# Attention's probabilities transposed by VectorE blocks and DRAM instead of TensorE, with the second half of each pair as a chain of its own

## The chip, the cores and the metric

One NeuronCore of a Trainium2 chip runs the whole program. The metric is the device time of one execution in microseconds; the median of three runs of the kernel before is 1203.68 us (1203.37 to 1203.94).

## What is computed

The reference has three stages; sizes are 2304 tokens (4 batches of 576), 512 features, 8 heads of 64.

```python
# 1. attention inside chunks of 64 tokens, for every head
scores = scale * np.matmul(q_c, k_c.transpose(0, 1, 2, 4, 3))
scores = scores - np.max(scores, axis=-1, keepdims=True)
attn = np.exp(scores)
attn = attn / (np.sum(attn, axis=-1, keepdims=True) + 1e-09)
out = np.matmul(attn, v_c)
# 2. four experts (512 -> 1024 -> 512), weighted by p and summed
h = np.maximum(x @ w1[e], 0.0)
out += p[:, e:e + 1] * (h @ w2[e])
# 3. rms norm, then a gated unit (512 -> 1536 -> 512)
g = xn @ w_gate
silu = g * (1.0 / (1.0 + np.exp(-g)))
val = xn @ w_val
return (silu * val @ w_out)
```

## The kernel before, in words

Tokens are cut into 18 tiles of 128, and these into three sets of six (`NSET`, `TPS`). Six stages follow each other on TensorE: the experts ("moe") for sets 0, 1 and 2, then the gated unit ("glu") for sets 0, 1 and 2. A moe stage has eight blocks k = 0 to 7 (four experts, two blocks each). A block is two calls of `hidden` (line 779: seven products of six 128x384 matmuls, in banks named a_ps, b_ps, c_ps, d_ps, with sums on VectorE between them) and one `outer` (line 942: six output tiles o, twelve 128x512 matmuls each, each tile added into `acc` by VectorE at line 1343). A glu stage has three blocks of four `hidden` and one `second` (line 977: seven `mult` of 18 matmuls 128x256; GpSimd and ScalarE make its operands, `part`). fp32 products are made of three passes over a high and a low part (`PASSES`).

Attention of set 0 runs at the start, one tile at a time. The twelve tiles of sets 1 and 2 run as six pairs beside the moe stages of sets 0 and 1 (`attention_unit`, line 481): load q, k and v; scores on TensorE into two PSUM banks sc; softmax, which takes nine VectorE instructions, two exponentials on ScalarE and four multiplications on GpSimd; then for each tile four 128x128 transposes on TensorE (line 529) into a bank trA, which ScalarE copies to SBUF as aT (line 534); then the products pv of aT with v (line 556), which ScalarE copies into xr (line 582). Set 2's pairs start at block (1, 4), that is k = 4 of the moe stage of set 1.

The order of all work is fixed when the program is built. `Chains` keeps a clock that `work.tick` moves on by an estimate of TensorE's time after each group of matmuls; each chain is a generator that is stepped when the clock reaches its next time, and `work.pause(us)` is a wait on this clock. `work.force` drives one chain to its end at once. On the chip every engine executes its own list in order, and all DMAs of interest go through one list, that of SyncE (SP below). Apart from attention these chains matter here:

- `weights` and `fetch` load and split expert weights; `w1_load` (line 299) loads parts of split weights into the twelve slots of `w1p`. `store` and `store_q` (lines 280, 457) put split parts away in DRAM, and on SP they wait for the GpSimd subtraction that makes the part.
- `decode` (lines 393 to 424) makes fp32 from the 64-bit gate, value and output weights with six VectorE instructions and one GpSimd addition per tile; its raw loads (`fetch64`, line 388) wait on SP for the VectorE instruction that frees their buffer. `prepare` splits the decoded tiles.
- `spot(n)` (line 773) puts one VectorE instruction of `decode` (or of `x_sums`, when that is under way) at places between TensorE groups. During blocks (1, 4) to (1, 7) a flag `busy` leaves out the spots that aren't marked calm.
- `put_away` and `turn` (lines 1175, 1192) already transpose the normalised expert output in another way: one VectorE instruction transposes a 128x512 tile in blocks of 32x32 (line 1181), four DMAs put the blocks in place in DRAM (`blocks_out`, line 1164, pieces of 32 rows), and a later load brings them back.

At the last block of a moe stage, line 1316 forces the attention chain to its end before `hidden` goes on.

## Time and profile before

| | us |
|---|---|
| runs, median (lowest to highest) | 1203.68 (1203.37 to 1203.94) |
| the profiled execution, its own time | 1204.62 |
| its span, first to last instruction | 1202.8 |
| TensorE matmul busy | 1188.5 (99%) |
| VectorE, ScalarE, GpSimd busy | 838.0, 482.7, 724.3 |
| DMA queue q1, share of 16 engines | 75.0% |

The profiled execution took 0.94 us more than the median; its span leaves out 1.8 us around the first and last instruction. The busy share of TensorE is an upper bound, since matmuls overlap and their ends are modelled: what one costs is read from the distance between starts. A wait is shown with the engine and line that ended it.

### The profile page before, as it was taken

How to read it: one execution, taken by the hardware profiler on the slowest of the kernel's cores; microseconds unless marked ns; L12 is line 12 of the kernel's file. 1: busy time of each engine (PE TensorE's matmuls, PEld its weight loads, DVE VectorE, ACT ScalarE, POOL GpSimd, SP SyncE). 2: the span in 40 equal slices, each digit the busy share in tenths (PEclk: the TensorE clock that was granted, in tenths of full speed). 3: DMA queues.
4: the chain of work that ended last, by engine and by line, in shares of the span. 5: the costliest groups of instructions: out<-in, count | busy, mean ns of one | idle time of the engine just before them, and what ended most of it. 6: DMA issues, size and time to landing. Idle time of an engine off the chain costs nothing.

```text
span 1202.8 us, 22161 instructions
## 1 busy us (share of the span) xinstructions
PE 1188.5 (99%) x7668; PEld 1109.1 (92%) x7668; DVE 838.0 (70%) x1456; ACT 482.7 (40%) x1116; POOL 724.3 (60%) x776
## 2 busy tenths in 40 slices
PE   8999999999999999999999999999999999999998
PEld 7888889999999988899999999999999999999998
DVE  5765544457678877779779888885687646774657
ACT  6445443333234334433344333344724243244322
POOL 4697666664476736547767776666337645385344
PEclk9999999999999999999999999999999999999999
DMA  8477655554679998576879998847998897688685
GB/s 262 145 265 248 232 193 201 193 189 149 208 243 322 321 311 293 185 242 203 287 257 305 294 304 298 307 169 238 315 289 252 290 323 239 228 282 294 216 292 178
DMA packets 190432, 302.47 MB, mean 251 GB/s; under 512 B 55280, under 2 KB 62960, under 8 KB 190320
## 3 DMA queue, kind: packets, MB, share of 16 engines
q1 hardware_dynamic: 189744, 300.53, 75.0%
q8 instruction: 61, 1.00, 0.3%
q10 hardware_dynamic: 576, 0.52, 0.1%
q14 instruction: 51, 0.42, 0.1%
HBM read 229.15 MB, written 71.83 MB: 250 GB/s over the span
## 4 chain that ended last, share of the span: by engine, by line
PE 91%; POOL 3%; DVE 2%; issue 1%; ACT 1%; DMA 1%; SPq 0%; DVEq 0%; POOLq 0%; ACTq 0%
PE o L956 30%; PE c_ps L726 14%; PE a_ps L726 14%; PE d_ps L726 14%; PE b_ps L726 7%; PE x L1006 7%; PE y L1006 3%; POOL w L201 1%; POOL tw L201 1%; PE pv L556 1%; DMA v<-in_qkv 1%; POOL hl L201 1%; PE sc L505 1%; PE trA L529 0%; ACT x L711 0%
## 5 line engine op out<-in xcount | busy, mean ns | idle before, releaser
L956 PE MATMUL o<-w,hh 128*128 128x512 f32 x1152 | 357.3, 391 | 0.6 <-POOL w L201 0.6
L201 POOL TENSOR_TENSOR w<-r,w 128x512 fp32r<-128x512 f32 (+1 forms) x146 | 168.9, 1164 | 151.1 <-ACT w L361 55.9
L956 PEld LDWEIGHTS o<-w,hh 128*128 128x128 f32 x1152 | 214.6, 188 | 44.2 <-POOL w L201 1.4
L956 PE MATMUL o<-w,hl 128*128 128x512 f32 x576 | 224.4, 390 | 0.0
L726 PE MATMUL c_ps<-x,w 128*128 128x384 f32 x1080 | 215.9, 337 | 1.0 <-DVE d_ps L202 1.0
L726 PE MATMUL a_ps<-x,w 128*128 128x384 f32 x984 | 198.0, 337 | 0.5 <-ACT p L787 0.5
L726 PE MATMUL d_ps<-x,w 128*128 128x384 f32 x984 | 197.2, 336 | 0.0
L726 PEld LDWEIGHTS c_ps<-x,w 128*128 128x128 f32 x1080 | 189.1, 188 | 2.0 <-DVE d_ps L202 1.6
L726 PEld LDWEIGHTS a_ps<-x,w 128*128 128x128 f32 x984 | 172.5, 188 | 3.3 <-ACT p L787 1.0
L726 PEld LDWEIGHTS d_ps<-x,w 128*128 128x128 f32 x984 | 173.0, 188 | 0.0
L1343 DVE SCALAR_TENSOR_TENSOR acc<-o,pr,acc 128x512 f32<-128x512 f32 x126 | 93.7, 747 | 111.9 <-PE o L956 111.8
L201 POOL TENSOR_TENSOR hl<-silu,hh 128x384 fp32r<-128x384 f32 x50 | 51.8, 1056 | 130.3 <-ACT hh L865 130.3
L956 PEld LDWEIGHTS o<-w,hl 128*128 128x128 f32 x576 | 108.1, 188 | 22.7
L201 POOL TENSOR_TENSOR w<-tw,w 128x256 fp32r<-128x256 f32 x136 | 112.5, 837 | 6.4 <-ACT w L236 5.9
L787 ACT COPY p<-a_ps 128x384 f32<-128x384 f32 x82 | 39.3, 480 | 155.0 <-PE a_ps L726 154.8
L726 PE MATMUL b_ps<-x,w 128*128 128x384 f32 x492 | 98.6, 336 | 0.0
L201 POOL TENSOR_TENSOR hl<-h_s,hh 128x384 fp32r<-128x384 f32 x70 | 73.8, 1076 | 40.3 <-ACT hh L865 20.8
L827 ACT ACTIVATE hh<-d_ps 128x384 fp32r<-128x384 f32 x92 | 45.3, 492 | 130.8 <-DVE d_ps L202 130.5
L202 DVE TENSOR_TENSOR u<-b_ps,p 128x384 f32<-128x384 f32 x82 | 45.4, 554 | 74.7 <-PE b_ps L726 54.3
L202 POOL TENSOR_TENSOR w<-w,sc 128x512 f32<-128x512 f32 x36 | 50.9, 1415 | 75.1 <-DVE sc L420 74.4
L236 ACT CAST w<-tw 128x256 fp32r<-128x256 f32 x136 | 51.9, 405 | 102.5 <-POOL tw L201 100.7
L1006 PE MATMUL x<-w,hh 128*128 128x256 f32 x480 | 91.3, 283 | 0.4 <-ACT x L711 0.4
(142 smaller groups left out, 1956.4 us busy)
## 6 DMA issues: line engine op xcount, KB each, us to landing
w<-wgv SPq DMA_DIRECT2D x252, 256.0 KB, 4.8
w<-w1m SPq DMA_DIRECT2D x224, 256.0 KB, 5.1
r<-in_w SPq DMA_DIRECT2D x128, 256.0 KB, 4.9
w<-wou SPq DMA_DIRECT2D x63, 512.0 KB, 5.9
w1m<-w SPq DMA_DIRECT2D x112, 256.0 KB, 3.2
wgv<-w SPq DMA_DIRECT2D x84, 256.0 KB, 4.8
raw<-in_wglu SPq DMA_DIRECT2D x36, 512.0 KB, 4.6
wou<-w SPq DMA_DIRECT2D x42, 256.0 KB, 3.9
```

What stands on the lines that cost most here:

```text
L201: sub = lambda eng, o, a, b: eng.tensor_tensor(o, a, b, op=ALU.subtract)
L202: add = lambda eng, o, a, b: eng.tensor_tensor(o, a, b, op=ALU.add)
L236: nc.scalar.copy(halves(out[n])[:, 0], at[part_of[n]])
L505: nc.tensor.matmul(sc[h2][c * CH:(c + 1) * CH, n:n + CH], q, k, start=True, stop=True)
L556: nc.tensor.matmul(ps[n][lo:lo + CH, o:o + CH], vt[a][row:row + CH, hp, c, :], aT[a][row:row + CH, q:q + CH], start=True, stop=True,)
L726: nc.tensor.matmul(ps[:, :NB], wv[:, wi, k, :], xs[n][:, xi, k, :], start=(first and k == 0 and m == 0), stop=(last and k == KH - 1 and m ...
L787: nc.scalar.copy(p1, v(a))
L827: nc.scalar.activation(hi, src, AF.Relu)
L956: nc.tensor.matmul(ps, hs[fps[k], b, j][hx][:, r * P:(r + 1) * P], w2[2 * k + j][:, wi], start=((k, j, m) == (0, 0, 0)), stop=((k, j, m) = ...
L1006: nc.tensor.matmul(ps[:, o:o + w], parted[fps[q], n][hx][:, t * P:(t + 1) * P], wv[:, q, wi], start=id(ps) not in opened, stop=(n in (1, 2 ...
L1343: nc.vector.scalar_tensor_tensor(out=acc[i], in0=ps, scalar=pr[:, i, e:e + 1], in1=acc[i], op0=ALU.mult, op1=ALU.add,)
```

## The change

The first six tiles keep the old way (`turned_here`). For the other twelve:

- VectorE transposes the tile of probabilities in 32x32 blocks into aq (one 128x512 instruction), four DMAs put the blocks into a new DRAM tensor `attd[i]` (pauses of 0.8 us between them instead of the 1.6 us of the other user), and a DMA loads aT from there.
- The load and what follows (pv and its copies) are a chain of their own, `attention_end`, so the next pair's scores can start before the pair has ended. It waits 2.5 us on the clock, loads the two aT, then waits 8 us more before pv.
- `placed=True`: a step of attention that wants VectorE is no longer taken when the clock is due; it is taken by `spot`, ahead of `decode`. The flag `busy` and the calm spots are gone. The row sums and the following two small instructions of softmax are now two steps.
- Set 2's pairs start at block (1, 2) instead of (1, 4), and `prepare` is slowed from there.
- At the last block of a moe stage, `force` also ends every chain in `ending`.
- In the very last `second`, three of the six closing additions go to GpSimd and all six are issued before `mult(1)`.

```diff
@@ -78,9 +78,9 @@
     def __init__(self):
         self.clock, self.rush, self.chains = 0.0, False, []
 
-    def add(self, gen, every=0.0, first=False, busy=None):
-
-        c = [gen, every, self.clock, every if busy is None else busy]
+    def add(self, gen, every=0.0, first=False, busy=None, placed=False):
+
+        c = [gen, every, self.clock, every if busy is None else busy, placed, None]
         self.chains.insert(0, c) if first else self.chains.append(c)
         return c
 
@@ -92,15 +92,18 @@
     def step(self, c, busy=False):
         c[2] = max(c[2], self.clock - 2.0) + c[3 if busy else 1]
         try:
-            next(c[0])
+            c[5] = next(c[0])
         except StopIteration:
             self.chains.remove(c)
+
+    def due(self, c):
+        return c[4] and c[5] is not None and "DVE" in c[5][0]
 
     def tick(self, us, busy=False):
         self.clock += us
         for c in list(self.chains) if not self.rush else ():
             for _ in range(2):
-                if c in self.chains and self.clock >= c[2]:
+                if c in self.chains and self.clock >= c[2] and not self.due(c):
                     self.step(c, busy)
 
     def race(self, runners, spare, idle):
@@ -182,6 +185,7 @@
     w1p = Slots(tc, ctx, "w1", 12, [P, 2, 2 * P], F32R)
     w2p = Slots(tc, ctx, "w2", 4, [P, 2, 512], F32R)
     r64 = Slots(tc, ctx, "r64", 2, [P, 1024], F32)
+    attd = {i: dram.tile([KD, P, P], F32, name=f"att_{i}") for i in range(TPS, NTILE)}
     xnt = [dram.tile([KD, P, NB], F32, name=f"xnt_{b}") for b in range(2 * NSET)]
     away = set()
     psum = ctx.enter_context(tc.tile_pool(name="psum", bufs=1, space=PSUM))
@@ -520,6 +524,23 @@
         yield from work.pause(5)
 
         aT = []
+        if done:
+            yield from turned_here(u, att, aT)
+            yield from attention_out(u, loaded, aT, d, done)
+            return
+        qs = []
+        for i, t in zip(u, att):
+            while not tp.free():
+                yield
+            yield {"DVE": 0.7}, 1
+            qs.append(tp.get(f"aq_{i}"))
+            nc.vector.transpose(qs[-1], t)
+            tp.put(t)
+            yield from work.pause(1.5)
+            yield from blocks_out(qs[-1], attd[i], 0, 0.8)
+        ending.append(work.add(attention_end(u, loaded, qs, aT, d)))
+
+    def turned_here(u, att, aT):
         for a, t in enumerate(att):
             yield {"PE": 0.45}, 1 + 2 * a
             while banks.free() < (1 if work.rush else 3) or not tp.free():
@@ -533,6 +554,22 @@
             yield {"ACT": 0.6}, 1
             nc.scalar.copy(aT[a], ps)
             banks.put(ps)
+
+    def attention_end(u, loaded, qs, aT, d):
+        yield from work.pause(2.5)
+        for i in u:
+            while not tp.free():
+                yield
+            aT.append(tp.get(f"aT_{i}"))
+            nc.sync.dma_start(out=aT[-1].rearrange("p (k n) -> p k n", k=HP), in_=attd[i].rearrange("k p n -> p k n"))
+            yield from work.pause(1)
+        yield from work.pause(8)
+        tp.put(*qs)
+        yield from attention_out(u, loaded, aT, d, None)
+
+    ending = []
+
+    def attention_out(u, loaded, aT, d, done):
         yield from work.pause(1)
         yield {"PE": 1.05 * len(u)}, 1
 
@@ -609,9 +646,10 @@
         yield {"ACT": d}, 1
         nc.scalar.activation(ex[1][:, :G * CH], ex[1][:, :G * CH], AF.Exp, scale=SCALE)
         for h2, e in enumerate(ex):
-            yield {"DVE": d + 0.6}, 3 - h2
+            yield {"DVE": d}, 3 - h2
             rs = sm.tile([P, G, 1], F32, tag="rs", name=f"rs_{h2}")
             nc.vector.tensor_reduce(rs, rows(e), axis=AX.X, op=ALU.add)
+            yield {"DVE": 0.6}, 1
             nc.vector.tensor_scalar_add(rs, rs, 1e-9)
             nc.vector.reciprocal(rs, rs)
             yield {"POOL": 0.65 * len(att)}, 1
@@ -768,13 +806,16 @@
             made_plain.pop(0)()
             catch_up()
 
-    decoding, adding, summing_up, busy = [], [], [False], [False]
-
-    def spot(n, calm=False):
-        for c in adding[-1:] if adding and adding[-1] in work.chains else decoding * (n if calm or not busy[0] else 0):
-            for _ in range(1 + summing_up[0]):
+    decoding, adding, summing_up = [], [], [False]
+
+    def spot(n):
+        for _ in range(n):
+            for c in adding[-1:] + [c for c in work.chains if work.due(c)] + decoding:
                 if c in work.chains:
                     work.step(c)
+                    if c in decoding and summing_up[0]:
+                        work.step(c)
+                    break
 
     def hidden(key, use):
 
...
@@ -1086,9 +1127,12 @@
         aside(2)
         spot(2)
         if last:
-            for o, y in (("c22", "y1"), ("c21", "y2")):
-                plus(nc.vector, o)
-                plus(nc.vector, y, high)
+            plus(nc.vector, "c22")
+            plus(nc.gpsimd, "c21")
+            plus(nc.vector, "y1", high)
+            plus(nc.gpsimd, "c12")
+            plus(nc.vector, "y2", high)
+            plus(nc.gpsimd, "y3", high)
             write("c22", both, 0, 1, (0, 1))
             write("y1", high, 0, 1, (2,), nc.scalar)
         mult(1, 0, 0, 0)
@@ -1099,8 +1143,6 @@
         spot(2)
         if last:
             take("y2", small[0], both)
-            plus(nc.vector, "c12")
-            plus(nc.vector, "y3", high)
             write("c11", both, 1, 0, (0, 1))
             write("y2", low, 1, 0, (2,), nc.scalar)
         mult(3, 6, 2 if last else 0, 1)
@@ -1161,7 +1203,7 @@
 
     scaled = []
 
-    def blocks_out(t, where, at):
+    def blocks_out(t, where, at, gap=1.6):
 
         rows = where.rearrange("k (j r) n -> r (k j) n", r=SQ)
         for g in range(P // SQ):
@@ -1169,7 +1211,7 @@
                 out=rows[:, :, at + g * SQ:at + (g + 1) * SQ],
                 in_=t[g * SQ:(g + 1) * SQ].rearrange("r (m c) -> r m c", c=SQ),
             )
-            yield from work.pause(1.6)
+            yield from work.pause(gap)
             yield
 
     def put_away(tiles):
@@ -1294,8 +1336,8 @@
                 if moe and (s, k) == (0, 1) and resting in work.chains:
                     work.force(resting, lambda: resting not in work.chains)
                 room[0] = 6 if k == 0 else 8 if k >= len(plan) - 2 else 0
-                if moe and (s, k) in ((0, 1), (1, 4)):
-                    ahead = work.add(attention(own(s + 1)), first=True)
+                if moe and (s, k) in ((0, 1), (1, 2)):
+                    ahead = work.add(attention(own(s + 1)), first=True, placed=True)
                 if (moe and s > 0 and k == 2) or (not moe and (s, k) == (0, 1)):
                     work.add(norm(s - 1 if moe else NSET - 1), 1.5)
                 if moe and s == 0 and k == 1:
@@ -1304,16 +1346,20 @@
                     work.add(fetch64())
                     decoding.append(work.add(decode(), 1e9))
                     preparing = work.add(prepare(), 1.0)
-                if moe and (s, k) in ((1, 4), (2, 0)):
-                    busy[0] = s == 1
+                if moe and (s, k) in ((1, 2), (2, 0)):
                     preparing[1] = 1.5 if s == 1 else 0.9
                 if k == len(plan) - 2 and not final:
                     if ahead is None:
                         ahead = work.add(turn(0 if moe else s + 1), 1.0)
                 if end and not final:
                     hold[0] = True
-                    if ahead in work.chains:
-                        work.force(ahead, lambda: ahead not in work.chains)
+                    for c in [ahead] + ending:
+                        if c in work.chains:
+                            work.force(c, lambda: c not in work.chains)
+                    for c in ending:
+                        if c in work.chains:
+                            work.force(c, lambda: c not in work.chains)
+                    ending.clear()
                     summing = work.add(x_sums((5,) if moe else (5, 6, 2)), 1e9 if moe else 0.8)
                     if moe:
                         work.step(summing)
```

`hidden` and `outer` lose the calm argument of `spot` and are otherwise unchanged. How this moves instructions is shown at three places.

TensorE, before: the end of the last `hidden` of block (1, 6) and the start of its `outer`, with the transposes (trA) of the last pair, tiles 16 and 17. In these names w is a part of the weights, x the split input, o an output tile, at the probabilities.

```order
L726 MATMUL d_ps<-x_3720,w_2_6118 128x384 x6
L726 MATMUL c_ps<-x_3732,w_3_6129 128x384 x6
L529 MATMUL trA_6346<-ident,at_6200 128x128 x4
L956 MATMUL o_6364<-w_6140,hh 128x512 x2
L956 MATMUL o_6364<-w_6140,hl 128x512
L956 MATMUL o_6364<-w_6205,hh 128x512 x2
L956 MATMUL o_6364<-w_6205,hl 128x512
L529 MATMUL trA_6372<-ident,at_6201 128x128 x4
L956 MATMUL o_6383<-w_6140,hh 128x512 x2
```

TensorE in the changed kernel: the end of the same `outer` and what follows it; no trA stands there, and pv of tiles 16 and 17 (aT_6462, aT_6464) comes after the last matmul of the block.

```order
L997 MATMUL o_6443<-w_6202,hh 128x512 x2
L997 MATMUL o_6443<-w_6202,hl 128x512
L997 MATMUL o_6443<-w_6231,hh 128x512 x2
L997 MATMUL o_6443<-w_6231,hl 128x512
L593 MATMUL pv_6468<-aT_6462,v_5827 64x64
L593 MATMUL pv_6469<-aT_6462,v_5827 64x64
L593 MATMUL pv_6468<-aT_6464,v_5830 64x64
L593 MATMUL pv_6469<-aT_6464,v_5830 64x64
```

The two groups of transposes are gone, and pv has moved from the middle of this `outer` (after its third unit of six matmuls) to its end, where the changed kernel forces the chain (its line 1358).

SP in the changed kernel, around the loads of these two aT (L303 loads weight parts, L1210 is `blocks_out`, L392 loads a raw 64-bit tile, L461 stores split parts, L564 loads aT).

```order
L392 DMA raw<-in_wglu 128x512
L303 DMA w_1_6370<-w1m_3_140 128x512
L1210 DMA att_98<-aq_6372 32x16x32 x4
L392 DMA raw<-in_wglu 128x512
L461 DMA wou_141<-w_0_6392 128x512
L461 DMA wou_141<-w_5_6404 128x512
L564 DMA aT_6462<-att_97 128x4x128
L564 DMA aT_6464<-att_98 128x4x128
L461 DMA wou_141<-w_4_6425 128x512
L461 DMA wou_141<-w_6_6439 128x512
```

Before, none of the rows L1210 and L564 were here. The loads of aT stand behind a raw load, which waits for VectorE, and behind two stores, which wait for GpSimd.

VectorE, before: the last `hidden` of block (1, 6), with the second half of softmax (e, rs) of the last pair between the sums of `hidden` (u, v, d_ps, c_ps, and hl, the low part).

```order
L202 TENSOR_TENSOR c_ps<-c_ps,u_6131 128x384
L830 SCALAR_TENSOR_TENSOR hl<-d_ps,hh 128x384
L614 TENSOR_REDUCE rs_6253<-e_6198 128x8
L615 TENSOR_SCALAR rs_6253<-rs_6253 128x8
L616 RECIPROCAL rs_6253<-rs_6253 128x8
L830 SCALAR_TENSOR_TENSOR hl<-c_ps,hh 128x384
L614 TENSOR_REDUCE rs_6272<-e_6199 128x8
L615 TENSOR_SCALAR rs_6272<-rs_6272 128x8
L616 RECIPROCAL rs_6272<-rs_6272 128x8
L202 TENSOR_TENSOR u_6279<-b_ps,p_6262 128x384
L202 TENSOR_TENSOR v_6291<-d_ps,u_6279 128x384
L202 TENSOR_TENSOR d_ps<-c_ps,v_6291 128x384
```

VectorE in the changed kernel, at the same instructions of softmax of that pair; they now lie at the end of block (1, 5) and in the next `hidden`.

```order
L651 TENSOR_REDUCE rs_6134<-e_6034 128x8
L206 TENSOR_TENSOR u_6148<-b_ps,p_6132 128x384
L206 TENSOR_TENSOR v_6163<-d_ps,u_6148 128x384
L206 TENSOR_TENSOR d_ps<-c_ps,v_6163 128x384
L653 TENSOR_SCALAR rs_6134<-rs_6134 128x8
L654 RECIPROCAL rs_6134<-rs_6134 128x8
L871 SCALAR_TENSOR_TENSOR hl<-d_ps,hh 128x384
L414 SCALAR_TENSOR_TENSOR w_6023<-raw,w_6023 128x512
L206 TENSOR_TENSOR d_ps<-d_ps,v_6163 128x384
L871 SCALAR_TENSOR_TENSOR hl<-a_ps,hh 128x384
L206 TENSOR_TENSOR c_ps<-c_ps,u_6148 128x384
```

Before, seven instructions of softmax stood between d_ps of one `hidden` and u of the next, with c_ps and two hl among them; now one row sum stands ahead of u, v and d_ps, and its two small instructions behind them.

## Rows read from the trace of the kernel before

**Rows 1.** Page, part 4: the chain that ended last, by engine
```profile
PE 91%; POOL 3%; DVE 2%; issue 1%; ACT 1%; DMA 1%; SPq 0%; DVEq 0%; POOLq 0%; ACTq 0%
```

**Rows 2.** Waits of TensorE: waiter, releaser, total us, times, longest us
```profile
PE c_ps L726 <- DVE d_ps L202: 1.0, 1, 1.0
PE x L1006 <- POOL hl L201: 1.0, 1, 1.0
```

**Rows 3.** Timeline of TensorE, 84.4 to 87.6: start us, us, instruction, count
```profile
85.25 0.62 PE L956 MATMUL o<-w,hh 128*128 128x512 f32 x2
...
85.93 0.60 PE L529 MATMUL trA<-ident,at 128*128 128x128 f32 x4
...
87.07 0.62 PE L956 MATMUL o<-w,hh 128*128 128x512 f32 x2
```

**Rows 4.** Timeline of TensorE around pv of the first and second pair
```profile
90.74 0.39 PE L956 MATMUL o<-w,hl 128*128 128x512 f32 x1
...
93.05 0.50 PE L956 MATMUL o<-w,hh 128*128 128x512 f32 x1
...
123.39 0.39 PE L956 MATMUL o<-w,hl 128*128 128x512 f32 x1
...
124.80 0.50 PE L956 MATMUL o<-w,hh 128*128 128x512 f32 x1
```

**Rows 5.** Timeline of TensorE in block (1, 6), 494 to 501
```profile
494.51 1.20 PE L726 MATMUL d_ps<-x,w 128*128 128x384 f32 x6
...
495.55 1.20 PE L726 MATMUL c_ps<-x,w 128*128 128x384 f32 x6
...
497.80 1.21 PE L726 MATMUL d_ps<-x,w 128*128 128x384 f32 x6
500.02 1.14 PE L726 MATMUL c_ps<-x,w 128*128 128x384 f32 x5 [1.02 <-DVE d_ps L202]
```

**Rows 6.** Timeline of VectorE and TensorE at the end of the program
```profile
1196.08 0.68 DVE L202 TENSOR_TENSOR out_c<-out_c,out_u 128x512 f32<-128x512 f32 x1
...
1197.02 0.68 DVE L202 TENSOR_TENSOR out_c<-x,out_c 128x512 f32<-128x512 f32 x1
...
1198.55 0.41 DVE L202 TENSOR_TENSOR out_y<-y,out_y 128x256 f32<-128x256 f32 x1
...
1197.09 0.88 PE L1006 MATMUL y<-w,p 128*128 128x256 f32 x6
```

**Rows 7.** Tile xq: duration ns min/median/max, first and last start; DMA landing
```profile
L1168 SPq DMA_DIRECT2D xnt<-xq x72: 303/428/3030, 373.9 to 922.6; - x72
L1181 DVE STREAM_TRANSPOSE xq<-acc x18: 694/701/711, 372.6 to 916.8; 128x512 f32<-128x512 f32 x18
...
DMA to landing us min/median/max: 1.8/4.7/8.7
```

**Rows 8.** Windows: us, busy of PE, PEld, DVE, ACT, POOL, PEclk, DMA share, GB/s
```profile
400.00:440.00 40.00, 40.00 (x260) 35.57 (x259) 33.85 (x60) 13.69 (x31) 25.78 (x29) 1.00 1.03 324
```

**Rows 9.** DMA issues, 480 to 520: count, KB each, median us to landing
```profile
w<-w1m SPq DMA_DIRECT2D x14, 256.0 KB, 5.0
...
raw<-in_wglu SPq DMA_DIRECT2D x2, 512.0 KB, 3.9
```

**Rows 10.** Lines of VectorE: count, busy us, mean ns, idle before
```profile
L1343 DVE SCALAR_TENSOR_TENSOR acc<-o,pr,acc 128x512 f32<-128x512 f32 x126 | 93.7, 747 | 111.9 <-PE o L956 111.8
...
L420 DVE SCALAR_TENSOR_TENSOR sc<-raw,sc 128x512 f32<-128x512 uint32 x36 | 28.3, 785 | 0.2
L418 DVE TENSOR_SCALAR sc<-w 128x512 uint32<-128x512 uint32 x36 | 23.9, 664 | 0.4
```

**Rows 11.** Waits of the SP queue: total us, times, longest us
```profile
SPq L299 <- PE a_ps L726: 85.0, 58, 17.0
...
SPq L388 <- DVE sc L420: 59.4, 15, 10.5
```

**Rows 12.** Lines of GpSimd: the addition that ends a decoded tile
```profile
L202 POOL TENSOR_TENSOR w<-w,sc 128x512 f32<-128x512 f32 x36 | 50.9, 1415 | 75.1 <-DVE sc L420 74.4 <-DMA w<-w1m 0.6
```

More of the change, by code (lines that the diff above doesn't have):

```diff
@@ L804, in hidden @@
         product(a, w(1), 1, False, True)
-        spot(1, True)
+        spot(1)
         catch_up()
@@ L809, in hidden @@
         product(d, w(2), 2, True, True)
-        spot(1, True)
+        spot(1)
         add(nc.vector, v(d), v(d), v4)
@@ L963, in outer @@
             work.tick(6 * 0.227)
-            spot(1 if n + 1 < len(order) else 0, k == 0)
+            spot(1 if n + 1 < len(order) else 0)
             aside(n)
```

## The prediction, made before the run

> **What bounds the kernel now.** I read first the chain of waits, by engine, to see who is last: TensorE holds 91% of it [rows 1]. Then the windows: in 400 to 440 us, where the attention of set 2 is under way, TensorE is busy 40.00 of 40 us at a granted clock of 1.00, VectorE 33.85, GpSimd 25.78 and ScalarE 13.69 [rows 8]. Then TensorE's waits by releaser: nothing that matters here is over 1 us [rows 2]. So a matmul taken off TensorE is worth the distance between starts that it takes up, and what the other engines do costs nothing until it makes TensorE wait. Last the timelines, for those distances, and the waits of SP's queue, because the change puts new loads and their consumers into that list.
>
> The profiled execution is 0.94 us above the median. All terms are differences within it; I apply their sum to the median, 1203.68.
>
> **What comes off TensorE's path.**
>
> *Transposes.* Three 512-wide matmuls take 0.68 us from start to start; three with one group of four transposes among them take 1.14 (85.93 to 87.07) [rows 3]. A group costs 0.46 us. Twelve tiles, one group each: 12 × 0.46 = **−5.5**. Nothing excuses them: both stages around them hold TensorE full.
>
> By the row a transpose is 0.115 us of TensorE's time. The Trainium skill (VectorE: DVE Perf Modes, The three transpose paths, and Rules for kernel authors) speaks against this change: a 128x128 transpose belongs on TensorE, at 390 ns, since VectorE turns only 32x32 blocks. By its 390 ns, 48 transposes would be worth 18.7 us (an estimate), over three times what the row gives; the row was taken in this flow and decides.
>
> *pv of the first pair.* Around pv of the second pair the starts lie 1.41 us apart, around that of the first 2.31 [rows 4]. The same instructions, so 0.9 us of the first is a wait, for the copies that end just ahead of it. Now aT is loaded some 11 us of the planner's clock ahead (2.5 for the first, 8 behind the last): **−0.9**. Ends: 0 and −0.9.
>
> *Softmax in block (1, 6).* c_ps follows d_ps by 1.04 us normally and by 2.22 where TensorE stands 1.02 for VectorE [rows 5]. There seven softmax instructions stood together between the sums of two `hidden`; in the new order they are apart and placed by `spot`. **−1.2**; ends 0 (another cluster takes its place) and −1.2.
>
> *The last `second`.* Two closing additions on VectorE, at 1196.08 and 1197.02, follow each other by 0.94 us; the last one starts at 1198.55 [rows 6]. Three of six now go to GpSimd, so VectorE comes free sooner, but the last addition still needs TensorE's last six y matmuls, which end at 1197.09 + 0.88 = 1197.97. It can start about 0.1 later, 0.5 before 1198.55: **−0.5** (ends 0 and −0.5).
>
> Gains together: −5.5 − 0.9 − 1.2 − 0.5 = −8.1.
>
> **What it adds.**
>
> *The forced last pair.* At the start of block (1, 7) the chain of tiles 16 and 17 hasn't ended, so `force` puts its two loads and pv into the lists at once: on TensorE right behind the last matmul of the `outer` before, on SP behind a raw load and two stores. That raw load waits for a VectorE instruction that stands two places behind the adding of the fourth o tile: 0.747 + 0.664 + 0.785 = 2.2 us [rows 10] after that tile's last matmul. TensorE has two o tiles left then, 24 matmuls at 0.68/3 [rows 3]: 5.44 us. SP is free 3.2 us ahead of pv. It issues the raw load, two stores and the first aT at 0.43 us each [rows 7], 1.7 us, and the second aT load starts 1.5 us before pv is due. It moves 256 KB in pieces of 512 bytes a row; the nearest row is w1m, also 256 KB, landing 5.0 us after issue [rows 9]. TensorE waits 5.0 − 1.5 = **+3.5**. Bounds: 1.8, the shortest landing of the nearest tile, gives 0.3; 8.7, its longest [rows 7], with SP 2 us later still, gives about 9. I take the row of equal size.
>
> *Decode later.* Twenty-four row sums and their small instructions, and 12 transposes of 0.70 us [rows 7], stand at spots that decode had, and preparation is slowed from (1, 2) on. Decode and preparation therefore end some tens of us later, in the first block of glu, where GpSimd makes `second`'s operands. TensorE already waits 1.0 us there for hl [rows 2]. One addition of decode on GpSimd is 1.415 us [rows 12]; if it falls between the last pair of hl, TensorE waits that much more, elsewhere nothing. I take **+0.4**, between 0 and 2.
>
> *Counted as nothing.* The 12 VectorE transposes, 8.4 us over some 300: VectorE has 6 us free in 40 [rows 8], and they take the place of decode's instructions, so the sums of `hidden` aren't behind them more than before; without that cover each would show its 0.70. The 48 block stores and 12 loads on SP: 60 × 0.43 = 26 us of issue [rows 7], spread over six pairs; cover: SP spends 85 us waiting for TensorE to free weight slots [rows 11], so it is ahead of its consumers; without this cover see the third rival. The aT loads of the other five pairs: issued 10 to 11 us of the clock before pv, against 5.0 to land; one that landed at 8.7 would still be in time. The bytes: 12 × 256 KB, written and read, 6 MB beside 324 GB/s [rows 8], about 19 us of transfer; the engines show a share of 1.03 already, so weights will come later by some of it, again within SP's lead.
>
> **Sum:** −8.1 + 3.5 + 0.4 = −4.2: 1203.68 − 4.2 = **1199.5 us**.
>
> **The rivals.**
>
> *The last load is in time.* If SP reaches the aT loads 3 us earlier than I reckon, or they land like the fastest stores, the +3.5 goes: 1203.68 − 8.1 + 0.4 = **1196.0**. For it: 1.8 us was seen for this kind of transfer [rows 7]. Against: the DMA engines are full there [rows 8].
>
> *Waits eat the gain.* The block stores write 128-byte pieces. The rows show that they land slowly for their size: 64 KB in 4.7 us (median) against 256 KB in 5.0 [rows 7, 9]. A load of aT waits on SP until the last store has landed; for the forced pair that is a further few us, and pv stands for it: up to the bound of 9 instead of 3.5, and a us or two lost at other pairs. −8.1 + 0.4 + 7.5 = −0.2: **1203.5**.
>
> By that pair of rows a small piece costs some four times its bytes. The Trainium skill (DMA: Bandwidth & Descriptors, Specifications) says that below 512 bytes the engine reads, modifies and writes and doesn't reach line rate; by this rule the change's block stores are its weak place, and the rows agree.
>
> *SP's list falls behind (slower).* All goes through one list in order. In moe stage 1 each pair adds ten DMAs, 10 × 0.43 = 4.3 us, and its loads stand for the landing of block stores: 8.7 for the slowest against 0.8 + 2.5 + 1 = 4.3 of pauses between the last store and the second load, 4.4 us. Everything behind stands too, and that is expert weights. Their lead is the twelve slots, a slot a product of 1.04 us [rows 5]: 12 us, less 5 to 9 for landing. SP already waits up to 10.5 us for decode's VectorE instructions at raw loads [rows 11], and a decode that is displaced makes that longer. Once SP is more than some 6 us behind, TensorE stands for weights; 3 to 4 us at each of three pairs is +10 on the forecast: **1209.6**. For it: the stage is the densest of all. Against: the 85 us that SP waits for TensorE, 58 times [rows 11].
>
> That the change does nothing is excluded: in the new order trA is gone from the twelve tiles.
>
> **How the numbers follow.** A measurement can tell 0.2%, 2.4 us, from no change: faster is below 1201.3, slower above 1206.1. The forecast has 0.55; its own range is 1197.9 (the load landing half-way between 1.8 and 5.0, so a wait of 1.9) to 1201.6 (the pv and softmax gains, 2.1, both missing). The load in time has 0.17, for all of it depends on a lead of 3 us; waits that eat the gain 0.16; SP behind 0.12. Faster: 0.47 of the 0.55, whose upper end passes 1201.3, and all of 0.17, together 0.64. Slower: the 0.12. Same: the remaining 0.08 and the 0.16, together 0.24. The range leaves out the slower rival and some of both other ends: 1195.8 to 1203.5.
>
> **What would show it.** On TensorE: no trA in the later tiles and 0.68 us from start to start throughout (transposes). A wait of pv on a DMA of aT at the start of block (1, 7), 3.5 us; none at other pairs. The wait of c_ps for d_ps gone, or a new one of x, hl or c_ps elsewhere (softmax). Two hl waits or a longer one in the first `second` of glu (decode later). The last VectorE instruction 0.5 us earlier behind the last matmul (tail). Wrong would be: waits of TensorE for w in moe stage 1 (SP behind); aT waits at several pairs; or a granted clock under 1.00 behind a wait, of which nothing is in the sum.

## The result, and the profile after

The changed kernel takes 1215.14 us (median of five runs, 1212.61 to 1215.99) against 1203.46 of the kernel before: ratio 1.0092, interval 1.0081 to 1.0103. It is slower by 11.7 us, and outside the range of the prediction. The profiled execution took 1215.99 us, the longest of the five; its span is 1214.1.

The first view is the chain that ended last by engine, as in [rows 1].

```profile
PE 86%; POOL 5%; DMA 5%; issue 2%; DVE 1%; ACT 1%; SPq 0%; DVEq 0%; POOLq 0%; ACTq 0%
```

TensorE has lost 5 points to GpSimd and to DMAs. The waits of TensorE, as in [rows 2], say for what (waiter, releaser, total us, times, longest):

```profile
PE pv L593 <- DMA aT<-att: 5.6, 4, 3.1
PE a_ps L764 <- DMA w<-wgv: 4.2, 1, 4.2
...
PE x L1047 <- POOL hl L205: 1.9, 3, 1.0
PE a_ps L764 <- ACT p L828: 1.8, 2, 1.2
...
PE c_ps L764 <- DVE d_ps L206: 0.5, 1, 0.5
```

The waits for aT were forecast, at 3.5 for the forced pair. The wait for w<-wgv, a part of the gate's weights, was not.

**Where the time went.** TensorE runs the same 6402 matmuls of products in both kernels, in the same order, so the start of a matmul after, minus its start before, is how far the kernel lags there. The lag grows by these steps, from the two profiled executions (span 1202.8 before, 1214.1 after). Its rows are cut by the clock of the kernel before: the row of moe 1 goes from that stage's third block, at about 360 us, to 521, just behind the forced pair; the row 815 to 870 holds the end of glu's first block, with its `second` from 827 to 842, and nearly all of the second block's `hidden`. Below, and in the texts recorded before the runs, this stretch is called glu's first block.

| | us |
|---|---|
| start, to 22 us | +0.95 |
| moe 0 and on to 360 (set 1's pairs) | -3.92 |
| 360 to 521, moe 1 (set 2's pairs) | +3.99 |
| 521 to 815, moe 2 | +0.02 |
| 815 to 870, glu set 0, around the first `second` | +10.53 |
| 870 to the last matmul | -0.57 |
| behind the last matmul's start | +0.32 |
| sum | +11.32 |

The start differs between executions of the same code by as much (it lies between -0.87 and +0.95 below), and the -0.57 is one short gap in the profile of before, at 1060, that none of the other profiles has. What counts is the middle. The +10.53 is not a fixed size either: e10 below runs the same instructions in that stretch and lost 7.8 there.

*The gain is there.* TensorE after, at the place of [rows 3], without trA:

```profile
86.24 0.62 PE L997 MATMUL o<-w,hh 128*128 128x512 f32 x2
86.70 0.39 PE L997 MATMUL o<-w,hl 128*128 128x512 f32 x1
86.92 0.62 PE L997 MATMUL o<-w,hh 128*128 128x512 f32 x2
```

0.68 us from 86.24 to 86.92, where [rows 3] has 1.14. The lag falls by 0.44 to 0.48 at each of the twelve places. Six groups and the first pair's pv, 6 × 0.46 + 0.9 = 3.7, make most of the -3.92 of moe 0.

*Block (1, 7).* TensorE, the forced last pair (the last column is the wait ahead), and below it windows of the changed kernel (columns as in [rows 8]; the granted clock is the third from the end):

```profile
513.75 0.39 PE L997 MATMUL o<-w,hl 128*128 128x512 f32 x1
517.25 0.33 PE L593 MATMUL pv<-aT,v 64*64 64x64 f32 x4 [3.11 <-DMA aT<-att]
518.07 1.76 PE L593 MATMUL pv<-aT,v 64*64 64x64 f32 x60 [0.49 <-DMA aT<-att]
519.76 2.23 PE L764 MATMUL a_ps<-x,w 128*128 128x384 f32 x6
521.82 1.20 PE L764 MATMUL b_ps<-x,w 128*128 128x384 f32 x6
```

```profile
513.70:519.50 5.80, 2.20 (x64) 1.64 (x65) 0.75 (x1) 0.00 (x0) 0.30 (x1) 0.90 0.83 289
519.50:522.00 2.50, 2.50 (x19) 2.38 (x12) 0.00 (x0) 2.11 (x4) 0.00 (x0) 0.54 0.00 0
522.00:525.00 3.00, 3.00 (x19) 3.00 (x19) 1.67 (x3) 1.21 (x3) 1.30 (x1) 1.00 0.48 111
```

3.11 + 0.49 of waits, and then something that was not in the sum: behind them the granted clock is 0.54, near the lower of its two levels (1.2 GHz), until 522. The six matmuls of a_ps take 2.06 us from start to start instead of 1.04, the 60 of pv 1.69 instead of 1.08 (as at the fourth pair, 415.51 to 416.59). That is 1.6 us more. The SP queue ahead of it:

```profile
510.57 0.35 SPq L392 DMA_DIRECT2D raw<-in_wglu  x1
511.03 1.12 SPq L461 DMA_DIRECT2D wou<-w  x2
512.20 1.38 SPq L564 DMA_DIRECT2D aT<-att  x2
```

The raw load leaves 3.2 us ahead of the start of the last o matmul, the loads behind it, as worked out. Two other pairs wait too, 1.68 (at 415) and about 0.6 (at 482; 0.36 of it shows as a wait). At the first of them the second load left SP only 4.9 us ahead of pv, at 408.61, and landed at 415.47 (SP, then TensorE):

```profile
408.61 0.37 SPq L564 DMA_DIRECT2D aT<-att  x1
```

```profile
413.51 0.33 PE L593 MATMUL pv<-aT,v 64*64 64x64 f32 x4
415.51 1.15 PE L593 MATMUL pv<-aT,v 64*64 64x64 f32 x60 [1.68 <-DMA aT<-att]
```

*glu's first block.* GpSimd in the first `second`, after:

```profile
837.48 3.96 POOL L205 TENSOR_TENSOR hl<-silu,hh 128x384 fp32r<-128x384 f32 x4
841.39 1.29 POOL L206 TENSOR_TENSOR w<-w,sc 128x512 f32<-128x512 f32 x1
842.64 1.97 POOL L205 TENSOR_TENSOR hl<-h_s,hh 128x384 fp32r<-128x384 f32 x2
844.57 0.73 POOL L205 TENSOR_TENSOR tw<-w 128x256 f32<-128x256 f32 x1
...
851.65 0.74 POOL L205 TENSOR_TENSOR w<-tw,w 128x256 fp32r<-128x256 f32 x1
```

The addition of [rows 12] (L206, 1.29 us) lies between two groups of hl, and behind it comes the whole splitting of the last output weights, to 852. Before, GpSimd's last instruction of this splitting started at 802.14, ahead of the first `second`:

```profile
802.14 0.74 POOL L201 TENSOR_TENSOR w<-tw,w 128x256 fp32r<-128x256 f32 x1
```

Decode is 50 us late. The waits of its SP queue, between 836 and 872, as in [rows 11]:

```profile
SPq L461 <- POOL w L205: 7.3, 1, 7.3
```

and its TensorE then, with a window for the granted clock of the stretch behind:

```profile
858.33 1.20 PE L764 MATMUL c_ps<-x,w 128*128 128x384 f32 x6
863.73 2.26 PE L764 MATMUL a_ps<-x,w 128*128 128x384 f32 x6 [4.19 <-DMA w<-wgv]
865.78 1.55 PE L764 MATMUL d_ps<-x,w 128*128 128x384 f32 x6
```

```profile
863.70:867.40 3.70, 3.67 (x14) 3.70 (x15) 0.59 (x2) 0.28 (x1) 0.00 (x0) 0.62 1.05 395
```

SP stood 7.3 us at a store that waits for GpSimd; the loads of gate weights behind it came late, and all at once (DMA share 0.28 from 845 to 850, 1.02 to 1.06 from there to 867). Of the 10.5 us, 3.2 are short waits for d_ps, hh and hl before and in `second`, 1.5 a wait for p, 5.8 this wait with the slow clock behind it. The wait for p goes back to the same late splitting: in ScalarE's list the copy p stands behind casts of the split parts (L240), which wait 4.2 and 3.0 us for GpSimd (ahead of their starts at 842.71 and 846.16). The last two parts, 7.3 of the 10.5, fall into `hidden` of the second block.

### The profile page after: what moved, and what is told of

Same layout as the page of the kernel before. It is cut to its first block, busy times and chain, and to the rows that moved or that the text cites. A ratio compares the mean times of both kernels' runs of the same rounds, so it can differ in the third digit from the quotient of the medians.

```text
span 1214.1 us, 22153 instructions
## 1 busy us (share of the span) xinstructions
PE 1188.3 (98%) x7620; PEld 1108.7 (91%) x7620; DVE 844.2 (70%) x1465; ACT 474.8 (39%) x1104; POOL 723.5 (60%) x779
## 4 chain that ended last, share of the span: by engine, by line
PE 86%; POOL 5%; DMA 5%; issue 2%; DVE 1%; ACT 1%; SPq 0%; DVEq 0%; POOLq 0%; ACTq 0%
PE o L997 29%; PE c_ps L764 13%; PE a_ps L764 13%; PE d_ps L764 13%; PE b_ps L764 7%; PE x L1047 6%; PE y L1047 3%; POOL hl L205 2%; DMA aT<-att 2%; POOL w L205 1%; PE pv L593 1%; POOL tw L205 1%; DMA wou<-w 1%; DMA w<-wgv 1%; PE sc L509 1%
## 5 line engine op out<-in xcount | busy, mean ns | idle before, releaser
L206 POOL TENSOR_TENSOR w<-w,sc 128x512 f32<-128x512 f32 x36 | 47.4, 1317 | 104.9 <-DVE sc L424 95.5
L206 DVE TENSOR_TENSOR u<-b_ps,p 128x384 f32<-128x384 f32 x82 | 45.5, 555 | 78.1 <-PE b_ps L764 55.0
L240 ACT CAST w<-tw 128x256 fp32r<-128x256 f32 x136 | 51.5, 405 | 112.4 <-POOL tw L205 110.3
```

The lines of the kernel that those rows point to most:

```text
L206: add = lambda eng, o, a, b: eng.tensor_tensor(o, a, b, op=ALU.add)
L240: nc.scalar.copy(halves(out[n])[:, 0], at[part_of[n]])
```

## The experiments

Theory A: the loss is decode that ends inside glu's first block, plus waits for aT at pairs. The planner's clock tells without a chip where preparation ends; beside the start of the first `second` on that clock it stands at -33 before and +14 after. The traces put the runs in the same order: GpSimd's last split starts 24.8 us ahead of the first matmul of `second` before and 22.9 behind it after, 9.6 and 13.8 behind in e4 and e2, 69.8 behind in e11, and 9 to 29 ahead in e1, e3, e5, e6, e7 and e8. Each table line below is the lag against the kernel before, by steps, from the profiled executions (the start and the -0.57 are left out, so a line doesn't add up to the time); "end" is preparation's end against the first `second`. Times are medians; each ratio is to the kernel before in the same series.

| run | end | moe 0 | 360-521 | 521-815 | 815-870 | behind | us | ratio (interval) |
|---|---|---|---|---|---|---|---|---|
| changed | +14 | -3.9 | +4.0 | 0.0 | +10.5 | +0.3 | 1215.1 | 1.0092 (1.0081, 1.0103) |
| e1 | -35 | -4.0 | +4.9 | +13.7 | 0.0 | +0.3 | 1217.8 | 1.0110 (1.0096, 1.0124) |
| e2 | +6 | 0.0 | +1.5 | +1.6 | +5.6 | -0.5 | 1212.0 | 1.0064 (1.0051, 1.0076) |
| e3 | -33 | -2.8 | 0.0 | +0.4 | 0.0 | -0.4 | 1200.8 | 0.9967 (0.9955, 0.9979) |
| e4 | +1 | -4.0 | -2.1 | +2.3 | +4.3 | +0.1 | 1205.6 | 1.0008 (0.9999, 1.0016) |
| e5 | -17 | -4.0 | +3.5 | +3.9 | 0.0 | +0.3 | 1207.6 | 1.0031 (1.0019, 1.0044) |
| e6 | -12 | -1.3 | -1.1 | +2.3 | 0.0 | +0.6 | 1204.0 | 1.0000 (0.9992, 1.0009) |
| e7 | -11 | -3.7 | +9.4 | 0.0 | 0.0 | -0.4 | 1210.4 | 1.0050 (1.0038, 1.0063) |
| e8 | -12 | -3.6 | -1.9 | 0.0 | 0.0 | -0.5 | 1197.7 | 0.9947 (0.9935, 0.9959) |
| e9 | +14 | -4.0 | +6.7 | +0.4 | +5.8 | +0.3 | 1213.3 | 1.0077 (1.0063, 1.0090) |
| e10 | +14 | -4.0 | +4.1 | +0.6 | +7.8 | -0.4 | 1212.8 | 1.0071 (1.0056, 1.0085) |
| e11 | +50 | -0.2 | +0.2 | +1.6 | +11.1 | -0.5 | 1220.7 | 1.0139 (1.0125, 1.0153) |

The column 815-870 is the finding: nothing is lost where preparation ends 11 or more ahead of the first `second`, and 4.3, 5.6, 8 to 10.5 and 11 where it ends 1, 6, 14 and 50 behind (e9, also at 14 but with its stores moved, loses 5.8; e11 loses 4.6 more behind 870).

**e1, decode caught up at once.**

```diff
+                if moe and (s, k) in ((2, 0), (2, 3)):
+                    extra[0] = k == 0
...
-                    if c in decoding and summing_up[0]:
+                    if c in decoding and (summing_up[0] or extra[0]):
```

> The changed kernel with one edit: in blocks (2, 0) to (2, 2) a spot takes two instructions of decode instead of one, so decode and preparation end some 49 us of the planner's clock earlier (785 instead of 834; the kernel before has 791). Theory A (late decode: the 10.5 us that the changed kernel loses between 826 and 867 us come from decode and preparation ending about 50 us later than before, inside glu's first second, on GpSimd and on SP): 1215.1 - 10 = 1205, between 1203 and 1207, and no wait of TensorE for hl, p or w<-wgv between 820 and 870 beyond the 1.0 us of before. Theory B (the new placing or the DRAM traffic costs it there in another way): 1213 to 1217.

Measured: 1217.8. The loss in glu is gone, as A says, and 13.7 have come up in moe 2 in its place; the time is a miss for both. The waits of TensorE in e1 between 560 and 660:

```profile
PE a_ps L764 <- ACT p L828: 5.2, 3, 2.4
PE c_ps L764 <- DVE d_ps L206: 1.2, 2, 0.9
```

Timeline of VectorE in e1, in the `hidden` ahead of the longest of these waits (at 632.63):

```profile
624.65 0.70 DVE L414 SCALAR_TENSOR_TENSOR w<-raw,w 128x512 uint32<-128x512 uint32 x1
625.28 1.52 DVE L418 TENSOR_SCALAR sc<-raw 128x512 uint32<-128x512 uint32 x1
626.72 0.54 DVE L871 SCALAR_TENSOR_TENSOR hl<-d_ps,hh 128x384 fp32r<-128x384 f32 x1
627.18 1.51 DVE L420 SCALAR_TENSOR_TENSOR w<-sc,w 128x512 f32<-128x512 uint32 x1
628.73 0.43 DVE L422 TENSOR_SCALAR sc<-w 128x512 uint32<-128x512 uint32 x1
629.07 0.56 DVE L206 TENSOR_TENSOR d_ps<-d_ps,v 128x384 f32<-128x384 f32 x1
```

Two instructions of decode stand at each spot, the sum of `hidden` (d_ps) starts 4.4 us behind the first of them, ScalarE waits 2.27 for it with `hh`, and the copy p that TensorE needs is behind that in ScalarE's list. So VectorE's idle time in this stage is no cover for work put at the wrong place.

**e5, the same catching up, spread.**

```diff
+                extra[1] = moe and s == 2
...
-                    if c in decoding and summing_up[0]:
+                    extra[0] += c in decoding
+                    if c in decoding and c in work.chains and (summing_up[0] or extra[1] and extra[0] % 4 == 0):
```

> The changed kernel with one edit: in the whole of moe stage 2 every fourth instruction of decode brings the next with it, so preparation ends at 803 of the planner's clock (changed kernel 834, its first second starts at 820). Theory A (late decode costs some 10 us in glu's first block; the run with two instructions at every spot lost its gain only because it crowded them into three blocks): 1215.1 - 10 + 0 to 4 = 1205 to 1209. Rival D (what decode is late by costs VectorE's consumers as much wherever it is made good): 1213 or more.

Measured: 1207.6, 7.5 under the changed kernel, within A's range; 3.9 in moe 2 are the price, 10.5 in glu the gain. Rival D falls.

**e2 and e11, the kernel before with decode late and nothing else.** In e2 the flag `busy` is set from (1, 2), in e11 from (1, 1).

```diff
-                if moe and (s, k) in ((1, 4), (2, 0)):
+                if moe and (s, k) in ((1, 2), (2, 0)):
                     busy[0] = s == 1
+                if moe and (s, k) in ((1, 4), (2, 0)):
```

> The kernel before with one edit: the flag busy is set from block (1, 2) on instead of (1, 4), so decode leaves out spots for two more blocks and preparation ends at 830 of the planner's clock instead of 791 (the changed kernel: 834). Transposes and attention are those of before. Theory A (late decode): 4 to 10 us slower than before, 1207.5 to 1213.5, with waits for hl and for w<-wgv in glu's first block. Theory B: as before, 1203 to 1205.

> The kernel before with the flag busy set from block (1, 1) on: preparation ends at 874 of the planner's clock, 50 behind the start of the first second (before: 33 ahead of it; with the flag from (1, 2): 6 behind, 5.6 us lost between 815 and 870). Theory A (the loss grows with how far decode reaches into glu): over 10 us lost between 815 and 900, 1215 to 1230. Rival (only the work that falls within the first second costs): 5 to 8 lost there, 1209 to 1213.

Measured: 1212.0 and 1220.7, both in A's ranges. No transpose was touched. By lateness alone e2, 6 behind, loses 5.6 in glu's first block (and 1.5 and 1.6 in moe 1 and moe 2), e11, 50 behind, 11.1 there and 4.6 behind it; the changed kernel's 10.5 lies between. The waits of TensorE in e2 are of the same two kinds as in the changed kernel:

```profile
PE x L1006 <- POOL hl L201: 3.0, 4, 1.3
...
PE a_ps L726 <- DMA w<-wgv: 1.2, 1, 1.2
...
PE b_ps L726 <- DMA w<-wgv: 0.9, 1, 0.9
```

**e3, set 1 only.** The transposes and the separate end go into the kernel before, for tiles 6 to 11 (the edit is shown against the change's own line).

```diff
-        if done:
+        if done or u[0] >= 2 * TPS:
             yield from turned_here(u, att, aT)
```

> The kernel before with VectorE's transposes, the DRAM path and the separate end for the six tiles of set 1 alone; set 2, decode's spots, the starts of the pairs and the closing additions are those of before. Theory A (the transposes pay, and the loss comes from what they push back): the gain that the changed kernel shows in moe stage 0, 4.1 us, and nothing else: 1199.4, between 1198.5 and 1200.5. Rival C (blocks and DRAM traffic cost as much as they save, through waits for aT or weights): 1202.5 or more.

Measured: 1200.8, 3.8 under the kernel before of its series (1204.6), 0.3 outside A's interval in absolute time. By steps the gain in moe 0 is 2.8, not the 4.1 forecast: two short waits, 0.4 at 83 us and 0.4 for aT, took some of it. The transposes pay for these six tiles.

**e4, the last pair on TensorE,** in the changed kernel.

```diff
-        if done:
+        if done or u[0] == NTILE - 2:
             yield from turned_here(u, att, aT)
```

> The changed kernel with tiles 16 and 17 transposed on TensorE as before. If the forced loads of aT cost what the trace shows: 3.6 us of waits, 0.7 in pv and about 1.4 of low granted clock behind them go and two groups of transposes, 0.9, come back: 4.8 less. Preparation ends 13 us of the clock earlier (821 instead of 834), still inside glu's first second; by theory A (late decode) that takes away 0 to 5 more: 1205 to 1210.5. If the forced wait hides other work (rival), 1213 or more.

Measured: 1205.6, in A's range, but by larger steps than forecast: 6.1 less in moe 1 (forecast 4.8) and 6.2 less in glu (at most 5), with 2.3 given back in moe 2. A single pair moved both losses, since decode's end moved too (+14 to +1).

**e6 and e7, placing alone and transposes alone.** e6 is the changed kernel with all tiles transposed on TensorE:

```diff
-        if done:
+        if True:
             yield from turned_here(u, att, aT)
```

e7 is the kernel before with the change's `attention_unit`, `turned_here` and `attention_end` (not its two steps of row sums), `attd`, the gap of `blocks_out` and the forcing of `ending`:

```diff
-                    if ahead in work.chains:
-                        work.force(ahead, lambda: ahead not in work.chains)
+                    for c in [ahead] + ending:
+                        if c in work.chains:
+                            work.force(c, lambda: c not in work.chains)
...
```

> The changed kernel with all twelve tiles transposed on TensorE and pv following in the same chain: the new placing, starts and closing additions are left, VectorE's transposes, the DRAM path and the separate end are not. Preparation ends at 812 of the planner's clock, 12 before the first second. Theory A (loss = late decode + waits for aT): neither is here, so 1203.5 - 1.2 (softmax) + 0.3 (closing additions), 1202 to 1205. Rival E (the placing itself costs): 1207 or more.

> The kernel before with VectorE's transposes, the DRAM path and the separate end for all twelve tiles, everything else as before. Preparation ends at 808 of the planner's clock, 11 before the first second; the last pair is forced as in the changed kernel. Theory A: -5.5 - 0.9 for the transposes and the first pv, + 3.6 + 0.7 + 1.4 for the forced pair with the low granted clock behind it: 1203.5 - 0.7, between 1201.5 and 1205. Rival F (the DRAM traffic of the blocks costs by itself): 1208 or more.

Measured: 1204.0, in A's range, and 1210.4, a miss by 5 that lies in rival F's range. In e6 the sum hides two steps that A did not name: 2.4 gained up to 521 and 2.3 lost in moe 2, mostly at waits for VectorE's sums. In neither does glu lose anything: each part alone moves preparation's end by about 20 of the clock, to 12 or 11 ahead of `second`, and only both together pass it. F is not the cause: moe 0, with half of the DRAM traffic, gains 3.7, and e8 below, with ten tiles, gains 3.6 there and 1.9 more in moe 1. The miss of e7 is the forced pair, which from the later start (1, 4) has still its transposes and eight block stores to do when it is forced (timeline of TensorE in e7):

```profile
509.43 0.40 PE L990 MATMUL o<-w,hl 128*128 128x512 f32 x1
521.24 0.57 PE L590 MATMUL pv<-aT,v 64*64 64x64 f32 x4 [11.41 <-issue]
```

11.4 us instead of 3.1: what a forced chain costs is the whole of its latency that is left.

**e9, stores later,** in the changed kernel.

```diff
-        yield from work.pause(2.5)
+        yield from work.pause(12)
         nc.sync.dma_start(out=where, in_=part.bitcast(F32))
```

> The changed kernel with one edit: a split part is stored 12 us of the clock after its GpSimd subtraction is planned instead of 2.5, so that on SP the stores of the last output weights stand behind the loads of gate weights that follow, not ahead of them. GpSimd's work is as late as in the changed kernel (833.6). Theory G (of the 10.5 us lost in glu's first block about 6, the wait for w<-wgv and the low clock behind it, come from SP standing 7.3 us at a store that waits for GpSimd): 3 to 6 us less there, 1209 to 1212, and no wait of a_ps for w<-wgv. Rival H (the DMA engines are full there, share 1.03, whatever the order): the wait stays, 1214 or more.

Measured: 1213.3, outside both ranges; the intervals of the ratios overlap, so by the time alone e9 can't be told from the changed kernel. By steps G holds: in glu 5.8 instead of 10.5 (7.8 in e10), and no wait for w<-wgv is left though GpSimd is as late as in the changed kernel. Rival H, full DMA engines, falls for this wait. What is left there is the waits for GpSimd, direct and, for p, by ScalarE's list. Most of the gain went at the forced pair: TensorE was there 3.8 us earlier, but the loads left at 514.03 instead of 512.20, behind four moved stores and the last block stores (timeline of TensorE in e9):

```profile
517.62 0.48 PE L593 MATMUL pv<-aT,v 64*64 64x64 f32 x4 [7.26 <-DMA aT<-att]
```

**e10, the old closing additions,** all on VectorE at their old places, in the changed kernel.

```diff
-            plus(nc.vector, "c22")
-            plus(nc.gpsimd, "c21")
-            plus(nc.vector, "y1", high)
-            plus(nc.gpsimd, "c12")
-            plus(nc.vector, "y2", high)
-            plus(nc.gpsimd, "y3", high)
+            for o, y in (("c22", "y1"), ("c21", "y2")):
+                plus(nc.vector, o)
+                plus(nc.vector, y, high)
...
             take("y2", small[0], both)
+            plus(nc.vector, "c12")
+            plus(nc.vector, "y3", high)
```

> The changed kernel with the six closing additions of the kernel before (all on VectorE, at their old places). Read from the trace: from the start of TensorE's last matmul to the end of the span, 5.41 us in the changed kernel and 5.11 before. Theory I (GpSimd's additions hold up VectorE's: out_y 128x256 took 1.51 us beside them against 0.41): 5.1 again and no VectorE addition of 128x256 over 0.5 us. Rival (the tail is set by the stores alone): 5.4. The time itself within 1 us of the changed kernel, 1214 to 1216.

Measured, from the start of the last matmul to the end of the span: 4.7, against 5.4 in the changed kernel; the runs with the old additions have 4.6 to 5.1, those with the new 5.2 to 5.7. The total, 1212.8, is 2.4 lower than the changed kernel's and 1.2 under what was expected; 0.7 of that is the closing, the rest (a shorter wait for w<-wgv, 2.6 instead of 4.2, and the start) is not part of the edit. Timeline of VectorE in the changed kernel:

```profile
1204.62 1.51 DVE L206 TENSOR_TENSOR out_y<-out_y 128x256 f32<-128x256 f32 x1
1206.05 1.51 DVE L206 TENSOR_TENSOR out_y<-out_y,out_y 128x256 f32<-128x256 f32 x1
```

GpSimd beside it in the changed kernel:

```profile
1204.09 3.19 POOL L206 TENSOR_TENSOR out_c<-out_c,out_u 128x512 f32<-128x512 f32 x2
```

and VectorE in e10:

```profile
1200.76 0.41 DVE L206 TENSOR_TENSOR out_y<-out_y 128x256 f32<-128x256 f32 x1
...
1201.69 0.41 DVE L206 TENSOR_TENSOR out_y<-out_y,out_y 128x256 f32<-128x256 f32 x1
```

The same additions take 0.41 alone and 1.51 while GpSimd adds. The Trainium skill has this rule (SBUF — State Buffer, Who interferes with whom): a VectorE instruction with two inputs in SBUF contends with a GpSimd one that reads SBUF, since its second input comes through the read interface that the two engines share. The trace agrees, at 1.1 us for each of these two additions.

**e8, ten tiles.** e7 with the last pair on TensorE and set 2's pairs, with the flag `busy`, from (1, 3).

```diff
-        if done:
+        if done or u[0] == NTILE - 2:
...
-                if moe and (s, k) in ((0, 1), (1, 4)):
+                if moe and (s, k) in ((0, 1), (1, 3)):
...
-                if moe and (s, k) in ((1, 4), (2, 0)):
+                if moe and (s, k) in ((1, 3), (2, 0)):
```

> The kernel before with VectorE's transposes and the DRAM path for ten tiles (not 16 and 17), set 2's pairs and the flag busy from block (1, 3) on; spots, softmax and closing additions as before. Preparation ends at 808 of the planner's clock, 12 before the first second. Theory A: the gain of set 1 alone, 3.8, and four more groups of transposes, 1.8, without a forced wait: 1198 to 1200. Rival (late decode costs already when it ends just ahead of second, or the loads of aT are late): 1201 or more.

Measured: 1197.7, 6.3 under the kernel before of its series, faster than both kernels and 0.3 under what was expected. TensorE is busy through glu's first block at full clock (a window of e8, columns as in [rows 8]):

```profile
800.00:870.00 70.00, 70.00 (x456) 69.87 (x456) 41.57 (x79) 39.21 (x86) 38.40 (x46) 1.00 0.85 284
```

## Why the prediction was wrong

The step that failed is "Decode later", a term of the sum put at +0.4 with bounds of 0 and 2. Its direction was right (decode and preparation end 50 us later, around the first `second` of glu, on GpSimd); it measured 10.5 in the profiled execution and 7.8 in e10's. I priced one addition of 1.415 us falling between two hl, put "elsewhere nothing", and stopped there. What was left out is the rest of the chain: behind that addition comes the splitting of the tiles, and the lists of two other engines stand still for it. SP waits at a store (7.3 us) with the next weights behind it, which cost 5.8; ScalarE waits at casts with p behind them, 1.5; the direct waits, the only kind that was priced, made 3.2. For the forced pair I had listed what is queued behind a waiting instruction, and got 3.5 for 3.6; here I had not. e2 and e11 show that lateness alone costs 5.6 and 11.1 there, e5 that making it good takes it away, e9 that SP's list is a part of it (4.7 less in glu than the changed kernel, 2.0 less than e10).

By the other steps:

- Transposes, -5.5: right. The lag falls by 0.46 at each tile; e3 and e8 turn it into time. The 390 ns that the prediction takes from the Trainium skill (VectorE: DVE Perf Modes, The three transpose paths) is that page's figure for bf16; these tiles are fp32, and the rows' 0.115 us decided.
- First pair's pv, -0.9: right, within what moe 0 shows. The wait goes with the path over DRAM alone (e7) and with the new placing alone (e6, -1.3 in moe 0 with every transpose still on TensorE).
- Softmax in block (1, 6), -1.2: right. c_ps follows d_ps by 1.04 there now (495.56 to 496.60, against [rows 5]), and the wait of 1.0 in [rows 2] is not there any more. It is also gone in e7 and e8, whose softmax and spots are those of before but whose pairs lie elsewhere, so that the new placing is what removes it is not shown.
- The last `second`, -0.5: wrong in sign, +0.3 in the profiles and 0.7 worse than the old additions in e10. The additions that stayed on VectorE became slower beside those moved; I had counted only their number.
- The forced last pair, +3.5: waits of 3.6, as worked out, but with 1.6 of low granted clock behind them. The prediction named a granted clock under 1.00 as something not in its sum; it came behind each of the long waits.
- "Counted as nothing", the loads of the other five pairs: two of them were late, 1.68 and about 0.6. The lead is what failed: their second loads left SP 4.9 and 5.9 us ahead of pv, not the 10 to 11 of the planner's clock, and landed after 6.9 and 6.5. With 10 us both would have been in time.
- "Counted as nothing", VectorE's transposes: 0.70 each as in [rows 7], and no wait is put down to one. What they cost is the spots: decode's lateness again.

Together: -8.1 became -7.6 + 0.3; +3.5 became 3.6 + 1.6 + 2.3; +0.4 became 10.5. That is 10.7 of the 11.3 that the profiles differ by.

The rival "SP's list falls behind" forecast the sign and named one of the two queues, with 0.12. It put the loss into moe stage 1, with a landing of block stores as its cause; no wait for expert weights is in the trace, the loss was two stages later, and SP stood for GpSimd. As a mechanism with a place it is not what happened, though SP was some 4 to 5 us behind its plan there, which cost the 2.3 at two aT loads; what held it there stays open. "The last load is in time" falls at the forced wait of 3.6. Of "Waits eat the gain" a us or two at other pairs came true (2.3), but the forced wait did not grow, and block stores that land slowly are not what made the loads late.

## What to carry to other kernels

Work that fills gaps (here decode) has a deadline, and what pushes it back is free until the deadline and then is not: two parts of a change that each cost nothing there can pass it together. So for displaced work look up when it ends now, how much slack it has, and what stands behind its last instruction on every queue, SP's stores above all. An idle share of an engine is not a cover; a place is.

## What the runs showed of the hardware

- TensorE's granted clock fell behind its long waits: 0.54 (519.5 to 522) behind 3.6 us, 0.62 (863.7 to 867.4) behind 4.2, and in e7 0.50 for 521 to 524 and 0.77 to 527 behind 11.4. It added 1.4 to 1.6 us in the changed kernel's two cases. Behind the wait of 1.68 at the fourth pair no such fall showed: its a_ps took 1.15 from start to start. At 2.6 it went either way: 0.60 (828 to 832) behind the wait of 2.56 for hl in e4, 1.00 (860.8 to 864) behind the 2.6 for w<-wgv in e10. So the price of a wait is not read from its length alone.
- GpSimd beside VectorE made a 128x256 addition take 1.51 us instead of 0.41.
- The block stores of attention land in 3.2 us (median, 1.8 to 5.4), faster than the 4.7 of the same stores of xnt in [rows 7], so the pieces of 128 bytes were not the weak place that the prediction made of them (tile aq of the changed kernel):

```profile
L1210 SPq DMA_DIRECT2D att<-aq x48: 302/448/1393, 97.1 to 506.2; - x48
L537 DVE STREAM_TRANSPOSE aq<-at x12: 696/701/702, 94.6 to 504.0; 128x512 f32<-128x512 f32 x12
...
DMA to landing us min/median/max: 1.8/3.2/5.4
```
